# One more warm-up matmul ahead of the first transposes, and a full-width filler behind them

## The chip, the cores and the metric

The kernel runs on one core of one Trainium2 chip. The metric is device time in microseconds of a whole execution; it is some 1.9 us more than the span that a profile shows. All runs told of here come from several batches ("calls" in what follows), on different chips; the kernels compared with each other ran in the same rounds of one call. Two kernels count as the same within 2%.

## The reference, cut to what matters

One block of a network: a layer norm of x (2048 rows, 512 columns), then a local dilated attention (32 heads, window 8, dilation 2) and a gated MLP with a spatial 2048 x 2048 product, both added to x.

```python
xn = _layernorm(x, axis=-1)
return x + _A_ref(xn, A_wqkv, A_wo) + _B_ref(xn, B_w_in, B_w_sp, B_b_sp, B_w_out)

# in _B_ref:
z  = _gelu(jnp.einsum('bsd,df->bsf', x, w_in))
z2 = _layernorm(z[..., Fh:], axis=-1)
```

Only the very start bears on the change: the first four blocks of 128 rows of x are normalised, transposed, and multiplied with the second half of B_w_in, which comes in four pieces of 128 rows.

## The kernel before: the parts that matter

The kernel lists its work as tasks, and a scheduler in the program fixes each engine's order from estimated times (`est`) before anything is built. The filler multiplies ones by ones into PSUM bank 7; nobody reads the result. Cuts are marked with dots.

```python
def filler(n, name, est, prio=None, reads=(), w=512):
    def warm(t):
        last = None
        for i in range(n):
            last = t.matmul(ps[:, 3584: 3584 + w], nc.const_aps.tensor(1.0, [128, 128], BF),
                            nc.const_aps.tensor(1.0, [128, w], BF), start=True, stop=True)   # L637
        return last
    T("pe", warm, reads=reads, writes=[("ps", 7)], est=est, name=name, prio=prio)

filler(cfg["warm"], "warm", 400.0 * cfg["warm"])          # warm = 8
...
# first_wave(): block 0 in two halves, centred only; the scale is applied later
for h in range(2):
    ce(0, 256 * h, 256, ("xc0", h), "ab"[h])               # VectorE, L681
    xt(0, (k0, k1)[h], (2 * h, 2 * h + 1), ("xc0", h), "ab"[h])   # TensorE transposes, L694
    T("act", ...)                                          # ScalarE eviction, L710
filler(cfg["fill0"], "fill0", 216.0 * cfg["fill0"], reads=(("xc0", 1),), w=256)
...
z2_mm(*u[0], (0, 1))            # block 0, needs pieces 0 and 1 of B_w_in, L935
xt(1, kx, range(4), "xc1")
...
z2_mm(*u[1], (0, 1))
z2_mm(*u[0], (2, 3))            # "the eight" begin here: need pieces 2 and 3
z2_mm(*u[2], (0, 1))
z2_mm(*u[3], (0, 1))
z2_mm(*u[1], (2, 3))
...
xt(2, k2, range(4), ("xn", 2))  # VectorE's normalised blocks 2 and 3, L676
...
xt(3, k, range(4), ("xn", 3))   # "the last transposes" in what follows
```

Blocks are counted from zero in this code; the texts written before the runs say "third block of x" for number 2 and "ninth" for number 8.

Of the kernel before, what the change touches and what calls it, by code (L numbers as in the profile page):

```python
# [14 lines left out]
class Plan:  # L15
# [299 lines left out]
    tmap=1,  # L315
    xdma=4,
    fill=1,
    warm=8,
    fill0=1,
    acc=1,  # L320
    first_plain=0,
# [3 lines left out]
def build_kernel(nc, A_x, A_wqkv, A_wo, B_x, B_w_in, B_w_sp, B_b_sp, B_w_out, out, report=False, sched_kw=None,  # L325
                 cfg=None, emit=True):
    cfg = dict(DEFAULT_CFG, **(cfg or {}))
# [71 lines left out]
    with ExitStack() as es:  # L399
# [120 lines left out]
        def c_act(n, psum=True, accum=False):  # L520
            return 165.0 + n * (0.84 if psum else 0.84) + (110.0 if accum else 0.0)

        def c_dve(n, mode=1.0):
            return 155.0 + n / (0.96 * mode)
# [3 lines left out]
        def T(eng, fn, **kw):  # L528
            t = plan.add(eng, fn, **kw)
            if eng == "pe" and not t.name.startswith(("warm", "fill", "xTr", "red")):  # L530
                pe_seq.append(t)
            return t
# [100 lines left out]
# [8 lines that stand above are left out]
# [21 lines left out]
        def first_wave():  # L662
            dv = []

            def bn(b):
                dv.append(T("dve", lambda v: v.bn_stats(Fv("st6", 6, 9 * b), A("xin", 512, 512 * b)), reads=[("xin", b)],
                            writes=[("st6", b)], est=690, name="bnst%d" % b))
# [39 lines left out]
            for h in range(2):  # L707
# [4 lines left out]
                    ps[:, 512 * (k0, k1)[h] + 256 * h: 512 * (k0, k1)[h] + 256 * h + 256].rearrange("p (c n) -> p c n", c=2),  # L712
                    ACTF.Copy))(h),
                  reads=[("ps", (k0, k1)[h])], writes=["xcT0" + "ab"[h]], est=c_act(256), name="xTe0" + "ab"[h])
            filler(cfg["fill0"], "fill0", 216.0 * cfg["fill0"], reads=(("xc0", 1),), w=256)
            bn(1)
            ag(1)
            ce(1, 0, 512, "xc1")
# [8 lines left out]
            for b in range(2):  # L727
# [7 lines left out]
              reads=[("ps", kx)], writes=["xcT1"], est=c_act(512), name="xTe1")  # L735
# [10 lines left out]
            for b, hf, k in u[2:]:  # L746
# [6 lines left out]
                reads=[("ps", k)], writes=[("xnT", 3)], est=c_dve(512), name="xTe3"))  # L753
# [326 lines left out]
        def v_wave(j):  # L1080
            for b in range(4 * j, 4 * j + 4):
                v_block(b)

        first_wave()
        setup_masks()
        qk_wave(0)
# [8 lines left out]
          reads=["bia"], writes=["bdf"], est=170, name="bdf")  # L1095
# [330 lines left out]
```

## Time and profile before

| | kernel before |
|---|---|
| time, median of the 3 first runs | 233.64 us (233.41 to 233.75) |
| span of the profiled execution | 231.0 us |
| TensorE busy, by the page | 226.5 us, 98% |

The chain of waits and TensorE's timeline are quoted in the prediction. Three points in time are enough to read every run below: when TensorE's array becomes fast, when the eight of L935 start, and when the last transposes of the first wave start (9.59 us in this profile). What "fast" means can be read from the starts of matmuls of 512 columns: among the warm-ups, from 1.22 to 3.78 us, they come (3.78 - 1.22)/6 = 0.427 us apart, and the 32 of L809, from 12.85 to 19.75 us, 0.216 us apart. The trace's record of the granted clock puts the change at 4.04 us. In the recorded texts "cold" is the slow spacing and "warm" the fast one.

One more view of this profile is the part of the timeline that shows VectorE (start, length, engine, line, operation, and in brackets the idle time before it with the releaser):

```profile
7.35 0.69 DVE L666 BATCH_NORM_STATS2 fpool<-arena 128x6 f32<-128x512 bf16 x1
7.95 0.40 DVE L676 TENSOR_SCALAR arena<-arena,fpool 128x512 bf16<-128x512 bf16 x1
8.27 0.19 DVE L670 BATCH_NORM_AGGREGATE fpool<-fpool 128x2 f32<-128x9 f32 x1
9.12 0.41 DVE L676 TENSOR_SCALAR arena<-arena,fpool 128x512 bf16<-128x512 bf16 x1 [0.67 <-POOL fpool L672]
```

### The profile page before, as it was taken

The numbers are of one execution on the slowest core, as the hardware profiler recorded it, in microseconds if no ns is written. First come the engines' busy times: TensorE is split into PE (matmuls) and PEld (weight loads), VectorE is DVE, ScalarE is ACT, GpSimd is POOL, SyncE is SP. The second block draws the span as 40 slices with busy tenths as digits, with TensorE's granted clock in tenths as the row PEclk, the third lists the DMA queues.
The fourth block names the chain that finished last, engine by engine and source line by source line (L and its number), as shares of the span: only waits on it lengthen the run. The fifth ranks groups of instructions, "written<-read, shape, count | busy, mean of one in ns | idle before, by whom it ended". The sixth has DMA issues, their size and how long they took to land.

```text
span 231.0 us, 3311 instructions
## 1 busy us (share of the span) xinstructions
PE 226.5 (98%) x1236; PEld 111.3 (48%) x1236; DVE 205.7 (89%) x237; ACT 129.3 (56%) x235; POOL 43.3 (19%) x74
## 2 busy tenths in 40 slices
PE   7999999999999999999999999999999999999995
PEld 2444445444434565555545454454544544544442
DVE  4688879998998999999999999999999989999920
ACT  3698658978889996447662243324423433255311
POOL 4647959628026001000000000000000000000000
PEclk9999999999999999999999999999999999999999
DMA  6995989784109200459618999999999664946082
GB/s 224 261 289 114 163 206 327 222 225 141 45 23 198 74 3 0 76 109 223 210 37 175 214 218 249 272 226 296 220 244 232 146 206 92 284 111 137 11 168 65
DMA packets 77887, 38.90 MB, mean 168 GB/s; under 512 B 66220, under 2 KB 76332, under 8 KB 76848
## 3 DMA queue, kind: packets, MB, share of 16 engines
q1 hardware_dynamic: 71488, 31.89, 60.7%
q10 hardware_dynamic: 5568, 4.69, 7.0%
q0 software_dynamic: 816, 2.12, 3.1%
q8 instruction: 9, 0.15, 0.3%
q14 instruction: 6, 0.05, 0.1%
HBM read 18.49 MB, written 4.21 MB: 98 GB/s over the span
## 4 chain that ended last, share of the span: by engine, by line
PE 96%; DMA 2%; SPq 1%; issue 0%; ACT 0%
PE ps L1159 37%; PE ps L1278 16%; PE ps L809 12%; PE ps L966 11%; PE ps L935 10%; PE ps L789 6%; PE ps L848 3%; DMA arena<-in_B_w_in_dram 2%; SPq L602 0%; PE ps L694 0%; SPq L611 0%; ACT arena L1120 0%
## 5 line engine op out<-in xcount | busy, mean ns | idle before, releaser
L1159 PE MATMUL ps<-arena 128*128 128x448 bf16 x448 | 90.6, 352 | 0.0
L1159 PEld LDWEIGHTS ps<-arena 128*128 128x128 bf16 x448 | 43.8, 98 | 42.8 <-ACT arena L1120 0.3
L1278 PE MATMUL ps<-arena 128*128 128x512 bf16 (+2 forms) x187 | 43.9, 366 | 0.0
L1227 DVE TENSOR_TENSOR arena<-arena 128x4096 bf16<-128x4096 bf16 x16 | 36.6, 2286 | 0.3
L835 DVE TENSOR_TENSOR arena<-arena 128x4096 bf16<-128x4096 bf16 x16 | 36.2, 2279 | 0.0
L1236 DVE TENSOR_TENSOR arena<-arena 128x4096 bf16<-128x4096 bf16 (+2 forms) x24 | 33.6, 1402 | 1.1 <-DMA arena<-arena 0.2
L1120 ACT ACTIVATE arena<-ps 128x512 bf16<-128x512 f32 (+2 forms) x23 | 13.0, 564 | 36.2 <-PE ps L1159 25.4
L809 PE MATMUL ps<-arena 128*128 128x512 bf16 x128 | 28.6, 379 | 0.0
L1278 PEld LDWEIGHTS ps<-arena 128*128 128x128 bf16 x187 | 17.9, 98 | 18.5
L935 PE MATMUL ps<-arena 128*128 128x448 bf16 x128 | 25.7, 352 | 0.5 <-issue 0.3
L966 PE MATMUL ps<-arena 128*128 128x448 bf16 x128 | 24.8, 353 | 0.0
L1052 DVE TENSOR_TENSOR arena<-arena 128x1024 bf16<-128x1024 bf16 x32 | 21.0, 683 | 0.3
L809 PEld LDWEIGHTS ps<-arena 128*128 128x128 bf16 x128 | 12.4, 98 | 15.3 <-issue 0.4
L966 PEld LDWEIGHTS ps<-arena 128*128 128x128 bf16 x128 | 14.4, 114 | 10.2 <-issue 0.8
L972 ACT ACTIVATE arena<-ps 128x896 bf16<-128x896 f32 x16 | 14.4, 915 | 8.7 <-PE ps L966 8.7
L817 ACT ACTIVATE arena<-ps 128x1024 bf16<-128x1024 f32 x16 | 16.3, 1021 | 4.5 <-PE ps L809 4.0
L935 PEld LDWEIGHTS ps<-arena 128*128 128x128 bf16 x128 | 12.2, 98 | 12.3 <-issue 0.6
L943 ACT ACTIVATE arena<-ps 128x448 bf16<-128x448 f32 x28 | 15.1, 549 | 2.1 <-PE ps L935 0.3
L977 ACT ACTIVATE arena<-arena 128x896 bf16<-128x896 bf16 x16 | 15.1, 945 | 0.1
L789 PE MATMUL ps<-arena 128*128 128x512 bf16 x64 | 15.0, 379 | 0.0
L1168 ACT ACTIVATE ps<-ps,fpool 128x448 f32<-128x448 f32 x16 | 9.7, 604 | 8.5 <-PE ps L1159 8.5
L1120 ACT ACTIVATE ps<-arena 128x512 f32<-128x512 bf16 (+2 forms) x17 | 9.8, 576 | 5.5 <-ACT arena L1120 5.1
(74 smaller groups left out, 200.4 us busy)
## 6 DMA issues: line engine op xcount, KB each, us to landing
arena<-vscr SPq DMA_DIRECT2D x8, 1152.0 KB, 6.6
arena<-in_A_x_dram ACTq DMA_DIRECT2D x18, 128.0 KB, 3.6
vscr<-arena POOLq DMA_DIRECT2D x16, 128.0 KB, 3.7
arena<-in_A_x_dram SPq DMA_DIRECT2D x14, 128.0 KB, 3.1
out_dram<-arena ACTq DMA_DIRECT2D x14, 128.0 KB, 2.4
arena<-in_A_wqkv_dram SPq DMA_DIRECT2D x3, 512.0 KB, 4.9
arena<-in_B_w_in_dram SPq DMA_DIRECT2D x1, 896.0 KB, 4.9
arena<-in_B_w_out_dram SPq DMA_DIRECT2D x1, 896.0 KB, 6.7
```

Of the source, the lines that this page charges most:

```text
L789: last = t.matmul(bank(k), AC(off["xnT"] + dc * S + 128 * b, [[1, 128]]), AC(off["wv_raw"] + 512 * dc, [[1, 512]]), start=(dc == 0), stop= ...
L809: last = t.matmul(bank(k + which), AC(off["wqk"] + 1024 * dc + col0, [[1, 128]]), AC(off["xnT"] + dc * S + 512 * j, [[1, 512]]), start=(dc ...
L817: T("act", lambda a: a.activation(AC(qo, [[ko - qo, 2], [1, 512]]), ps[:, 512 * k: 512 * k + 1024].rearrange("p (t n) -> p t n", t=2), ACT ...
L835: T("dve", lambda v: v.tensor_tensor(pbv, qb, kb, ALU.mult), reads=rd, writes=[("pb", s_)], est=c_dve(4096, 2.0), name="prod%d_%d" % (j, c ...
L935: last = t.matmul(ps[:, 512 * k: 512 * k + HF], AC(xo, [[1, 128]]), AC(off["w_in2"] + FH * dc + HF * hf, [[1, HF]]), start=(dc == 0), stop ...
L966: last = t.matmul(ps[:, 512 * (k + hf): 512 * (k + hf) + HF], AC(off["xnT"] + dc * S + t0, [[ts, 128]]), AC(off["w_in1"] + FH * dc + HF * ...
L1052: T("dve", (lambda o_, x_, y_: lambda v: v.tensor_tensor(o_, x_, y_, ALU.subtract))(o_, x_, y_), reads=rd, writes=[wr], est=c_dve(NK * 128 ...
L1120: T("act", lambda a: a.activation(out_, in_, ACTF.Copy), reads=reads, writes=writes, est=c_act(n), name=name)
L1159: last = t.matmul(half(bk), lh(k), rh(k), start=(new and k == 0), stop=(k == NK - 1), skip_group_check=True)
L1227: T("dve", (lambda tv, iv, av: lambda v: v.tensor_tensor(tv, iv, av, ALU.mult))(tv, iv, av), reads=[("attn", j)] + ([("Ve", par)] if q < 2 ...
L1236: T("dve", (lambda o_, n: lambda v: v.tensor_tensor(o_, two(0, n), two(n, n), ALU.add))(o_, n), reads=[] if n > 512 else ["Vs", ("Ve", par ...
L1278: last = t.matmul(po, lh, rh, start=False, stop=(q == len(order) - 1), skip_group_check=True)
```

## The change

The intent is that TensorE should not stand idle around the first transposes (0.40 us before them and 0.29 us before the first L935 in this profile), so that the array becomes fast early. That idle time there delays this moment, the profile before doesn't show.

```diff
-    warm=8,
+    warm=9,
...
-            filler(cfg["fill0"], "fill0", 216.0 * cfg["fill0"], reads=(("xc0", 1),), w=256)
+            filler(cfg["fill0"], "fill0", 216.0 * cfg["fill0"], reads=(("xc0", 1),))
```

## The prediction

> **What bounds the kernel now.** I started with the page's chain of work that ended last, because it says which engine a saved nanosecond has to be saved on.
>
> ```profile
> PE 96%; DMA 2%; SPq 1%; issue 0%; ACT 0%
> ```
>
> TensorE carries 96% of the span of 231.0 us, so the kernel is TensorE-bound; the DMA's 2% must be somewhere at an end. The same chain in order of time shows where:
>
> ```profile
> 1.71 0.42 SPq L602
> 2.14 0.04 issue
> 2.18 4.69 DMA arena<-in_B_w_in_dram
> 6.87 0.14 issue
> 7.00 1.67 PE ps L935 x8
> 8.68 0.22 PE ps L694 x4
> 8.90 0.76 PE ps L935 x4
> 9.66 0.33 PE ps L694 x4
> ...
> 217.90 10.40 PE ps L1278 x59
> 228.32 0.28 ACT arena L1120
> ```
>
> The reader is to see two things. Up to 6.87 us the path is not TensorE at all: it is the issues on the sync engine's queue and one load of B_w_in, issued at 2.18 and landed 4.69 us later. From 7.00 to about 228.3 us it is TensorE without a break. Whatever TensorE does before 7.00 us matters only if it makes the eight matmuls at 7.00 start later, or if it changes the speed of what follows. The change touches two instructions, and both lie before 7.00 us. So the third view is the timeline of TensorE alone for the first microseconds (start, length, what, and in brackets the idle time before it and who ended it):
>
> ```profile
> 0.84 3.45 PE L637 MATMUL ps<-const-bfloat16-1.0 128*128 128x512 bf16 x8 [0.84 <-PEq L1411]
> 4.69 0.39 PE L694 MATMUL ps<-arena 128*128 128x128 bf16 x4 [0.40 <-DVE arena L681]
> 4.92 0.27 PE L637 MATMUL ps<-const-bfloat16-1.0 128*128 128x256 bf16 x1
> 5.49 0.54 PE L935 MATMUL ps<-arena 128*128 128x448 bf16 x2 [0.29 <-issue]
> 6.05 0.40 PE L694 MATMUL ps<-arena 128*128 128x128 bf16 x4
> 6.28 0.54 PE L935 MATMUL ps<-arena 128*128 128x448 bf16 x2
> 7.00 1.67 PE L935 MATMUL ps<-arena 128*128 128x448 bf16 x8 [0.18 <-DMA arena<-in_B_w_in_dram]
> ```
>
> Line 637 is the filler: eight 512-wide matmuls of ones ahead of the first transposes (L694), and one 256-wide one behind them. TensorE stands idle 0.40 us before the transposes, which wait for VectorE's centred input (L681); 0.29 us before the first real matmuls (L935); and 0.18 us before the eight at 7.00. The list of all waits of TensorE has only these and the 0.84 us at the very start. The 0.29 us is put down to issue there, but the weight load that goes ahead of those matmuls starts at 5.45 and was released by the B_w_in transfer after 0.49 us of idle time. So that wait too is the load's.
>
> [...] Seven of the eight warm-up matmuls are recorded with 634 ns and the eighth, which starts at 3.78 us, with 511. The mean start-to-start time is (3.78 - 0.84)/7 = 0.420 us[...]. The four transposes and what follows start 4.92 - 4.69 = 0.23 us apart, 57 ns each, which is warm. So in this execution the speed doubled during the eighth warm-up matmul, near 4.0 us. [...]
>
> **The change part by part.** Nothing is removed. The order of instructions on each engine was compared for both kernels: TensorE has the same rows, with the warm-up nine times instead of eight and the later filler 512 wide; the other four engines are identical. The semaphores and the PSUM bank of the filler are the same.
>
> 1. The ninth warm-up matmul. In the profiled execution the eighth is recorded to end at 3.78 + 0.51 = 4.29 us, and some 0.17 us of that is drain (379 ns for a warm 512-wide matmul in the L809 row less 216 of spacing), so the next could start near 4.12. Warm, it occupies 0.22 us, to 4.34. If it were cold it would start at 0.84 + 8 x 0.427 = 4.26 and occupy 0.43, to 4.69. The transposes start at 4.69 in any case, because VectorE decides it. On the path: 0 us, with 0.35 us to spare warm and none cold.
> 2. The wider filler. [...] Its recorded end moves from 4.92 + 0.27 = 5.19 to about 5.30. The next weight load, released by the transfer, is at 5.45 and its matmul at 5.49. On the path: 0 us, with some 0.2 us to spare.
> 3. A shift that got through either place would still have the 0.18 us of waiting at 7.00 to disappear in. There is another small reserve at 9.59: the last of the four sets of transposes needs VectorE's L676, which ends at 9.12 + 0.41 = 9.53, while the matmuls before it were through streaming at 8.74 + 4 x 0.189 = 9.50.
> 4. The clock. In this execution it was fast from about 4.0 us on, three microseconds before the path reaches TensorE. Nothing is left to gain here.
>
> The sum for an execution like the profiled one is 0.00 us. TensorE's busy time should rise by about 0.5 us, and its idle time fall by the same.
>
> **The rivals.**
> - *A late clock in the timed runs.* [...] For it: the profiled execution took 233.02 us and the three timed ones 233.41 to 233.75, some 0.4 to 0.7 more[...]. Against it: the three agree within 0.34 us[...], and profiled and timed runs may differ for other reasons. This would give 232.9 to 233.4 us.
> - *The added work gets in the way.* If the clock is still slow at 4.7 us, nine warm-ups end just where the transposes want to start, and the filler holds TensorE 0.43 instead of 0.21 us[...]. Going through it cold from 4.69: transposes 4 x 0.107 to 5.12, filler to 5.55 instead of 5.33, so the matmuls start up to 0.1 us after 5.45. Two of those take 0.75, transposes 0.43, two more 0.75: 7.48 against 7.38 before. So 0.1 us later: 233.7 us. For it: only that the margin in a cold run is nil. Against: the profiled clock was fast.
> - *A second wait takes over.* Even if TensorE were ready earlier at 5.49 or 7.00, the B_w_in pieces end both waits, and their issue and transfers hang on nothing that TensorE does. So filling idle time cannot pull the path forward. This is the main line, 233.6 us.
>
> **Range and chances.** The main line says 233.64 us unchanged, and I give it some 65%. The late clock, at 25%, would take off about 0.5; the harmful case, at 10%, adds about 0.1. The weighted mean is 233.64 - 0.125 + 0.01, so 233.5. The scatter of the runs before is 0.34 us, so a new median can move by 0.2 without any cause. From the rivals' ends and this scatter, the range is 232.9 to 234.0 us. 2% is 4.7 us[...], so both outer chances are 0.5%; same is 99%.
>
> **What would show it right or wrong.** In the changed kernel's timeline the eight matmuls of L935 should still start near 7.0 us with a wait for B_w_in before them, and be gap-free after it; the wait before the first transposes should shrink from 0.40 to about 0.2 us and the one before the first L935 from 0.29 to about 0.2; the span should stay within 0.3 us of 231.0. I am wrong if the eight start later although the load landed at the same time (the added work got in the way), or if the time falls by over 0.5 us while the trace of before shows nothing to gain (the late clock was real in the timed runs), or if warm-up matmuls of 634 ns are seen beyond the eighth followed by slow matmuls after 7.00[...].

The sum came to 0.00 us. One of its terms is the time of the 256 further columns in step 2; half of the 0.216 us spacing of L809 puts it at 0.11 us, and as it lay beside the path it counted 0 in the sum. The first rival came to cost about 1 us at most, with which the 4.7 us of 2% were compared: that was the estimate and was not shown.

The other figures of the steps can be followed from the trace. The 0.427 us of step 1 is the slow spacing named above, and the second rival scales it by width: 0.107 us for 128 columns, 0.75 for two of 448. Later runs show both, 107 ns in the profile after (from 4.63 us) and 3.73 us for ten of 448 in warm5 (from 6.86 us). The 0.17 us that step 1 calls drain is what the recorded length in L809 (379 ns) exceeds the spacing by (216 ns).

## The result, and the profile after

The changed kernel took 233.72 us (median of 6 runs, 233.01 to 233.97); the kernel before took 233.52 us in 6 runs (232.88 to 234.32). The ratio is 1.0, with a 95% interval of 0.9975 to 1.0025: the same. Ratios here are the mean time of one kernel's runs over that of the other's in the same rounds, so they are not quite the ratio of the medians.

The span of the profiled execution is 231.2 us. First the busy line of the page, before and then after:

```profile
PE 226.5 (98%) x1236; PEld 111.3 (48%) x1236; DVE 205.7 (89%) x237; ACT 129.3 (56%) x235; POOL 43.3 (19%) x74
```

```profile
PE 225.9 (98%) x1221; PEld 111.7 (48%) x1237; DVE 206.2 (89%) x237; ACT 129.3 (56%) x235; POOL 42.8 (19%) x74
```

The weight loads show the added matmul (1237 against 1236). TensorE's busy time seems to fall by 0.6 us, but only because 16 matmul records are missing from the second trace (1221 for 1237 weight loads). So the rise of 0.5 us that I had named as a check can't be read from this line.

TensorE's timeline after, answering to the one in the prediction:

```profile
0.84 4.00 PE L637 MATMUL ps<-const-bfloat16-1.0 128*128 128x512 bf16 x9 [0.84 <-PEq L1411]
4.63 0.62 PE L694 MATMUL ps<-arena 128*128 128x128 bf16 x4
5.06 0.41 PE L637 MATMUL ps<-const-bfloat16-1.0 128*128 128x512 bf16 x1
5.73 0.55 PE L935 MATMUL ps<-arena 128*128 128x448 bf16 x2 [0.26 <-DMA arena<-in_B_w_in_dram]
...
7.23 1.69 PE L935 MATMUL ps<-arena 128*128 128x448 bf16 x8 [0.35 <-DMA arena<-in_B_w_in_dram]
...
9.73 0.39 PE L694 MATMUL ps<-arena 128*128 128x128 bf16 x4
```

The idle time before the transposes is gone, and what lies before the first L935 is a wait for B_w_in (0.26 us). The eight start 0.23 us later than in the profile before, and they still waited 0.35 us for their load. In the chain of waits after, the same load took longer:

```profile
2.18 5.00 DMA arena<-in_B_w_in_dram
```

It was 4.69 us before, from the same issue at 2.18 us. The load accounts for the whole shift of the eight: 0.31 us later landing against a start 0.23 us later. Of the 0.23 us, 0.09 us went in the reserve at the last transposes (9.73 against 9.59), and the span grew by 0.17 us. So no part of the later end, between these two traces, is the work of the fillers.

A second thing differs: the transposes start 5.06 - 4.63 = 0.43 us apart from the filler behind them, 107 ns each, where before it was 57. The array was still slow, and it became fast at about 5.1 us instead of 4.04. So more warm-up went with a later clock in this pair, which the experiments take up.

### The profile page after: what moved, and what is told of

Read it like the earlier page. It is cut to its first block, busy times and chain, and to the rows that moved or that the text cites. A ratio compares the mean times of both kernels' runs of the same rounds, so it can differ in the third digit from the quotient of the medians.

```text
span 231.2 us, 3297 instructions
## 1 busy us (share of the span) xinstructions
PE 225.9 (98%) x1221; PEld 111.7 (48%) x1237; DVE 206.2 (89%) x237; ACT 129.3 (56%) x235; POOL 42.8 (19%) x74
## 3 DMA queue, kind: packets, MB, share of 16 engines
q10 hardware_dynamic: 5568, 4.69, 6.7%
## 4 chain that ended last, share of the span: by engine, by line
PE 95%; DMA 2%; issue 1%; SPq 1%; ACT 0%
PE ps L1159 37%; PE ps L1278 16%; PE ps L809 12%; PE ps L966 11%; PE ps L935 10%; PE ps L789 6%; PE ps L848 3%; DMA arena<-in_B_w_in_dram 2%; SPq L602 0%; PE ps L694 0%; SPq L611 0%; ACT arena L1120 0%
## 5 line engine op out<-in xcount | busy, mean ns | idle before, releaser
L1278 PE MATMUL ps<-arena 128*128 128x512 bf16 (+2 forms) x178 | 42.1, 366 | 0.5
L835 DVE TENSOR_TENSOR arena<-arena 128x4096 bf16<-128x4096 bf16 x16 | 36.2, 2280 | 0.0
L809 PE MATMUL ps<-arena 128*128 128x512 bf16 x124 | 27.9, 379 | 0.4 <-issue 0.2
L935 PE MATMUL ps<-arena 128*128 128x448 bf16 x128 | 25.7, 353 | 0.6 <-DMA arena<-in_B_w_in_dram 0.6
L809 PEld LDWEIGHTS ps<-arena 128*128 128x128 bf16 x128 | 12.3, 98 | 15.4 <-issue 0.7
L935 PEld LDWEIGHTS ps<-arena 128*128 128x128 bf16 x128 | 12.2, 98 | 12.6 <-DMA arena<-in_B_w_in_dram 1.4
L789 PE MATMUL ps<-arena 128*128 128x512 bf16 x61 | 14.7, 379 | 0.3 <-issue 0.2
```

Of the source, the lines that this page charges most:

```text
L789: last = t.matmul(bank(k), AC(off["xnT"] + dc * S + 128 * b, [[1, 128]]), AC(off["wv_raw"] + 512 * dc, [[1, 512]]), start=(dc == 0), stop= ...
L809: last = t.matmul(bank(k + which), AC(off["wqk"] + 1024 * dc + col0, [[1, 128]]), AC(off["xnT"] + dc * S + 512 * j, [[1, 512]]), start=(dc ...
L835: T("dve", lambda v: v.tensor_tensor(pbv, qb, kb, ALU.mult), reads=rd, writes=[("pb", s_)], est=c_dve(4096, 2.0), name="prod%d_%d" % (j, c ...
L935: last = t.matmul(ps[:, 512 * k: 512 * k + HF], AC(xo, [[1, 128]]), AC(off["w_in2"] + FH * dc + HF * hf, [[1, HF]]), start=(dc == 0), stop ...
L1278: last = t.matmul(po, lh, rh, start=False, stop=(q == len(order) - 1), skip_group_check=True)
```

## The experiments

In every variant the order of each engine's other instructions was kept as in the kernel before and compared. Where the number of fillers changed by much, the estimate given to the scheduler stayed at that of eight, since otherwise work far behind moves too. The kernel before ran in the same rounds.

Two theories stood at the start. Mine: both additions lie beside waits that end when a load or VectorE says so. Rival 1 (late clock): in some executions the array becomes fast late, which costs time, and the change cures it. Rival 2: the added work gets in the way.

### The two halves of the change, each alone

```diff
 # warm_only
-    warm=8,
+    warm=9,
 # fill_only
-            filler(cfg["fill0"], ..., reads=(("xc0", 1),), w=256)
+            filler(cfg["fill0"], ..., reads=(("xc0", 1),))
```

> Only the ninth warm-up matmul is added; the filler behind the transposes stays 256 wide. Main theory (both additions lie beside waits for VectorE and for the load of B_w_in): time within 0.3 us of before, the eight matmuls of L935 start where that load lets them, near 7.0 to 7.2 us. Rival 1 (the array often becomes fast late in timed runs, and the extra matmul cures it): 0.3 to 0.5 us faster. Rival 2 (the extra matmul delays the transposes and the delay reaches the end): about 0.1 to 0.2 us slower, with the eight of L935 starting later than their load.

> Only the filler behind the first transposes is made 512 wide. Main theory: time within 0.3 us of before; the filler is through streaming by about 5.15 us warm or 5.5 us cold, and the next matmuls wait for the load of B_w_in to 5.45 us or later. Rival 2 (in the way): about 0.1 us slower. Rival 1 (late clock): no more than 0.1 us faster, as only 0.1 us of idle time is filled. [...]

The ninth warm-up alone took 233.52 us against 233.43 (ratio 1.0005, 0.9972 to 1.0039), the wide filler alone 233.61 us (1.0009, 0.9979 to 1.0038). Both are the same as before, as the main theory has it. The profiles bear it out: the eight of L935 started at 8.00 and 7.43 us after waits of 1.04 and 0.49 us, both ended by B_w_in (first warm_only, then fill_only):

```profile
8.00 1.67 PE L935 MATMUL ps<-arena 128*128 128x448 bf16 x8 [1.04 <-DMA arena<-in_B_w_in_dram]
```

```profile
7.43 1.69 PE L935 MATMUL ps<-arena 128*128 128x448 bf16 x8 [0.49 <-DMA arena<-in_B_w_in_dram]
```

The load landed at 7.91 us in the first, a whole microsecond later than in the kernel before, though nothing of the change touches it. The array became fast at 3.9 us with nine warm-ups and at about 5.5 us with eight, so here the smaller number was the later one. Each kernel also had one run over 235 us (235.34 and 235.20), of which more below.

### Next to no fillers

```diff
-        filler(cfg["warm"], "warm", 400.0 * cfg["warm"])
+        filler(1, "warm", 3200.0, w=64)
 ...
-            filler(cfg["fill0"], ..., w=256)
+            filler(cfg["fill0"], ..., w=64)
```

> Both fillers are cut to one matmul of 64 columns each, everything else in the same order. If the fillers earn their keep by having the array fast when the path reaches TensorE: the matmuls before 7 us run cold, the eight of L935 start near 7.4 us instead of 7.0[...]; worked out, 0.41 us of late start and half of the cold time after 7.4 us, less 0.1 us of reserve before the last transposes: 0.5 to 2.2 us slower, middle 1.1. Rival (the ramp costs nothing here, because the start is bound by loads and VectorE anyway): within 0.3 us of before.

The sum came to 0.5 to 2.2 us. That slow time costs half of itself is the two spacings' doing (0.427 and 0.216 us).

234.35 us against 233.43, ratio 1.0031 (1.0006 to 1.0056): slower by about 0.7 us, in the expected range. TensorE's timeline:

```profile
4.66 0.61 PE L694 MATMUL ps<-arena 128*128 128x128 bf16 x4 [3.60 <-DVE arena L681]
...
5.61 0.90 PE L935 MATMUL ps<-arena 128*128 128x448 bf16 x2 [0.30 <-ACT arena L710]
6.31 0.63 PE L694 MATMUL ps<-arena 128*128 128x128 bf16 x4
6.74 3.25 PE L935 MATMUL ps<-arena 128*128 128x448 bf16 x10
...
10.80 0.39 PE L694 MATMUL ps<-arena 128*128 128x128 bf16 x4
```

The two matmuls at 5.61 take 0.70 us to the next start, where the same two take 6.12 - 5.73 = 0.39 in the profile after, and the transposes at 6.31 start 107 ns apart instead of 57. Most of the ten at 6.74 are slow too. Ten at 189 ns (the spacing of the 16 of L935 from 9.82 us on in the profile before) would be 1.9 us to the next start; here it is 9.82 - 6.74 = 3.08 us. The last transposes start 1.21 us later than in the profile before and the span is 1.2 us longer; that profile is an early one among those with eight (table below), so the 0.7 us of the timed runs is the better measure. So the fillers as a whole do earn their keep here; one more of them doesn't (1.0005 for warm_only).

### Fewer and more warm-up matmuls

```diff
-        filler(cfg["warm"], "warm", 400.0 * cfg["warm"])
+        filler(16, "warm", 3200.0)      # warm16;  warm12 and warm5 with 12 and 5
```

> Sixteen warm-up matmuls instead of eight, order of all else frozen. This measures where added work stops being free. Eight or nine run cold, the rest at 0.216 us each, so the transposes start at 5.8 to 6.35 us instead of 4.69, the first L935 0.75 us after that, the eight 0.98 us after those: 7.5 to 8.1 us instead of 7.0. Less 0.1 us of reserve: 0.4 to 0.9 us slower, middle 0.6, and the eight of L935 no longer wait for the load. Rival (slack ahead of the path is over 1 us, or something later takes the delay up): within 0.3 us of before.

> Twelve warm-up matmuls instead of eight. With the array fast at 3.5 to 5.6 us the last streams until 5.0 to 5.9 us, the first L935 starts 0.75 us after that and the eight 0.98 us later: 6.7 to 7.6 us, where the load of B_w_in landed at 6.9 to 7.9 us. So most of four extra matmuls should still be hidden: 0.0 to 0.3 us slower in the mean. Rival (the added work of the change is hidden only just, with no room): four extra matmuls cost close to half of what eight extra did, 0.3 us, in every run.

> Five warm-up matmuls instead of eight, order of all else frozen. They end at 0.84 + 5 x 0.427 = 2.97 us, so TensorE idles 1.7 us before the transposes. If [...] (3.5 to 5.6 us in the runs with eight and nine, 9.0 us with next to none), the array becomes fast later than with eight, most likely between 5 and 9 us, and the time is 0.0 to 1.1 us higher, middle 0.5. Rival (idle time before the transposes has no influence, five are as good as eight): fast at 3.5 to 5.6 us again, time within 0.2 us of before.

Sixteen took 234.04 us against 233.43 (1.0018, 0.9995 to 1.0041), which doesn't clear the scatter, but the trace shows the added work on the path:

```profile
0.84 5.05 PE L637 MATMUL ps<-const-bfloat16-1.0 128*128 128x512 bf16 x16 [0.84 <-PEq L1411]
5.73 0.38 PE L694 MATMUL ps<-arena 128*128 128x128 bf16 x4
...
6.48 0.55 PE L935 MATMUL ps<-arena 128*128 128x448 bf16 x2 [0.26 <-ACT arena L710]
...
7.09 2.16 PE L935 MATMUL ps<-arena 128*128 128x448 bf16 x10
...
10.07 0.39 PE L694 MATMUL ps<-arena 128*128 128x128 bf16 x4
```

The transposes now follow the warm-up without a gap. (They start at 5.73 us, a little before the 5.8 that I had given as the earliest.) The ten of L935 run through with no wait for the load between them, and the last transposes come 0.48 us later than in the profile before; the span is 0.6 us longer. Profiles with eight and nine warm-ups scatter as widely, so it isn't the 0.48 us that decides, but the chain of waits of this profile, which now begins with the fillers and not with the load:

```profile
0.84 5.05 PE ps L637 x16
```

In this execution rival 2 is right, at eight matmuls more. What it costs is not shown by the times.

Twelve took 233.41 us against 233.88 (ratio 0.9961, 0.9928 to 0.9993). I don't read that as a gain: in this call the kernel before had five of its eleven runs over 234.3 us, and 233.41 is no lower than the kernel before in other calls (233.29 to 233.6). It shows that four more matmuls cost nothing that the timing sees, against the rival of that run. The profile of this kernel tells more. Its array became fast only at 6.62 us, so all twelve ran slowly, and the chain of waits begins with them too:

```profile
0.84 5.28 PE ps L637 x12
```

The ten of L935 started at 7.45 us, so the eight among them at about 7.83 (two at 189 ns later), past the 6.7 to 7.6 us that I had expected. So no fixed number of fillers is free: how many fit ahead of the load depends on when the array becomes fast (at 3.74 us in warm16, 6.62 in warm12) and on when the load lands (at 6.87 us in the profile before, 7.91 in warm_only).

Five took 234.61 us against 233.88, with runs from 233.80 to 235.90 (ratio 1.0012, 0.9969 to 1.0056): undecided by time. In its profile the array became fast only at 11.02 us, later than the 5 to 9 us that I had expected, the last transposes started at 11.78 us, and the span was 233.1 us. That the rival's "five are as good as eight" fails is shown for this execution only.

### The two kernels once more

No edit: the kernel before and the changed one, as they are, for more profiles and times.

> The kernel before, unchanged, for a second profile and more times. Main theory: what differs from run to run is when the last piece of B_w_in and the later rows of x land (6.9 to 7.9 us for the former in the four profiles so far) and when the array becomes fast (3.5 to 5.4 us so far); the last four transposes of the first wave then start at 9.6 to 10.5 us, and the span is 221.4 us more than that, within 0.1 us unless another wait appears later. Rival (the scatter arises later in the kernel): spans that do not follow the start of the last transposes.

> The changed kernel, unchanged, for a second profile and more times. Main theory: same time as before within 0.3 us, the last transposes between 9.6 and 10.5 us and the span 221.4 us more. If the extra fillers fixed the moment at which the array becomes fast, it would be at 5.0 us again as in the first profile of this kernel[...].

In the same rounds before2 took 233.29 us and after2 233.26 (ratios to the kernel before of those rounds, 0.9991 and 0.9989). All profiles together, sorted by when the array became fast:

| run | warm-ups | array fast at | last transposes at | span | span less last transposes |
|---|---|---|---|---|---|
| early_load (below) | 8 | 3.46 | 10.95 | 232.3 | 221.4 |
| warm16 | 16 | 3.74 | 10.07 | 231.6 | 221.5 |
| warm_only | 9 | 3.90 | 10.49 | 231.9 | 221.4 |
| before | 8 | 4.04 | 9.59 | 231.0 | 221.4 |
| after3 (below) | 9 | 4.22 | 9.81 | 231.6 | 221.8 |
| decouple (below) | 8 | 4.76 | 9.80 | 232.3 | 222.5 |
| after2 | 9 | 4.87 | 9.44 | 231.6 | 222.2 |
| after | 9 | about 5.1 | 9.73 | 231.2 | 221.5 |
| fill_only | 8 | about 5.5 | 9.93 | 231.8 | 221.9 |
| before2 | 8 | 5.57 | 9.67 | 231.1 | 221.4 |
| warm12 | 12 | 6.62 | 10.43 | 231.9 | 221.5 |
| tiny_both | 1 small | 8.96 | 10.80 | 232.2 | 221.4 |
| x4_first (below) | 8 | 10.17 | 11.42 | 234.7 | 223.3 |
| warm5 | 5 | 11.02 | 11.78 | 233.1 | 221.3 |

The moments come from the trace's own record of the granted clock; for the two with "about", which lack it, from the spacing and length of the matmuls. (In the windows view that clock stands as 1.00 even for stretches where matmuls ran at the slow spacing, for instance from 3.34 to 6.76 us in x4_first, so it is the spacing that has to be read.) Two things follow. With eight warm-ups the moment lies at 3.5 to 5.6 us in five profiles and at 10.17 in a sixth (x4_first), with nine at 3.9 to 5.1 us in four: they overlap, so the number alone doesn't fix it. And nine of the fourteen spans are 221.3 to 221.5 us plus the start of the last transposes, whatever came before: from there on these nine run alike.

The other five lost 0.3 to 1.9 us more later on. My expectation for after2, a constant 221.4 us, failed by 0.8 us (its last transposes, at 9.44 us, also came before the 9.6 that I had given). The wait list of TensorE in that run shows one of the places, the reduction matmuls of L848 waiting for VectorE's products:

```profile
PE ps L848 <- DVE arena L835: 0.3, 1, 0.3
```

VectorE starts its second wave (L768) when later blocks of x land. In after2 it waited until 12.42 us for that, against 12.20 in before, and twice more for DMA transposes (0.51 and 0.68 us); its first L835 started at 24.52 instead of 23.34 us. So which chain ends last changes from run to run, in the same kernel.

### The last piece of B_w_in earlier

```diff
 # sync engine's queue
-   ldx0, ldw_in2_0, ldx2, ldw_in2_2
+   ldx0, ldw_in2_0, ldw_in2_2, ldx2
```

> The last piece of B_w_in is issued ahead of the third block of x on the sync engine's queue (they change places), nothing else. If TensorE's start hangs on that load alone, as the chain of waits has it: the eight of L935 start 0.2 to 0.5 us earlier than in the kernel before and the time falls by as much. My theory is that a second chain is as long: the rows of x, through VectorE's statistics and normalisation (L666 to L676), to the last transposes at 9.6 us and later. Then the third block of x lands later by about 0.4 us (224 KB at some 390 to 400 GB/s are 0.57 us, less what was in flight), its statistics start no earlier than 6.7 us, the last L676 ends no earlier than before, and the time is the same or up to 0.5 us slower, though the eight start earlier.

The 390 to 400 GB/s are from the windows view of the profile before: 399 from 3.6 to 4.0 us, 390 from 4.0 to 4.3, 396 from 5.0 to 5.5.

234.36 us against 233.60, ratio 1.0039 (1.0011 to 1.0067): slower by about 0.9 us, where I had allowed for 0.5 at most. TensorE's timeline and the load that VectorE waited for:

```profile
7.18 1.67 PE L935 MATMUL ps<-arena 128*128 128x448 bf16 x8 [0.50 <-DMA arena<-in_B_w_in_dram]
9.78 0.40 PE L694 MATMUL ps<-arena 128*128 128x128 bf16 x4 [0.92 <-DVE arena L676]
...
7.59 0.69 DVE L666 BATCH_NORM_STATS2 fpool<-arena 128x6 f32<-128x512 bf16 x1 [1.46 <-DMA arena<-in_A_x_dram]
```

The eight did not start earlier (7.18 us; both theories had expected that), so the load was not hastened in effect. But the third block of x landed at 7.57 us, its statistics began 1.35 us later than in before (6.24 us; I had expected some 0.4 us, and why it was so much more stays open), and TensorE then stood 0.92 us for L676. That is the second chain, shown as a bound by itself: with it late, an array that was fast from 3.46 us on is of no use.

### Both chains eased by order

```diff
 # TensorE: u[0] (2, 3) after u[2] (0, 1) and u[3] (0, 1)
-   z2_0_0_2, z2_1_0_0, z2_1_1_0, z2_0_1_2
+   z2_1_0_0, z2_1_1_0, z2_0_0_2, z2_0_1_2
 # VectorE
-   bnst3, norm2, bnag3, norm3
+   bnst3, bnag3, norm2, norm3
```

> Two changes of order alone, aimed at both chains: TensorE does the four matmuls of the second block that need only the first two pieces of B_w_in ahead of the two that need the last piece, and VectorE closes the fourth block's statistics (L670) before it normalises the third block, so that GpSimd's power runs beside the normalisation. If the two chains are the bound: the last L676 ends about 1.4 to 1.5 us after the fourth L666 began to be followed up, some 0.2 us earlier than in the kernel before, TensorE's wait for the load shrinks to 0.1 us or less, the last transposes start 0.05 to 0.2 us earlier, and the time is 0.0 to 0.3 us lower, which the timing can hardly show. If neither is the bound: no change of the last transposes' start.

233.33 us against 233.60, ratio 1.0001 (0.9974 to 1.0028): nothing gained. The wait before the eight was 0.31 us and was now ended by ScalarE's eviction (L733), not by the load, so the 0.1 us that I expected failed too. From the start of the fourth block's L666 to the end of the last L676 it took 9.60 - 7.54 = 2.06 us against 9.53 - 7.35 = 2.18 before; the saving was 0.12 us instead of 0.2. No version here beats the two kernels.

### A misjudged move, and a late clock

```diff
 # sync engine's queue
-   xTd0, ldx8, xTd1, ldx4, ldx5, ldx6, ldx7, ldwv, ...
+   xTd0, ldx4, xTd1, ldx5, ldx6, ldx7, ldwv, ldx8, ...
```

> On the sync engine's queue the fifth block of x is issued in the place where the ninth was, and the ninth after the V weights; nothing else. In the second profile of the changed kernel and in that of the reordered kernel, TensorE lost another 0.5 to 0.8 us after 12 us, with VectorE waiting for the fifth block to 12.4 and 13.1 us and L848 waiting for VectorE's L835. If that third chain (x block five, VectorE, first products) is a bound in some runs: the first L768 starts at 11.5 us or earlier instead of 12.2 to 13.1, TensorE has no wait for L835 at L848, the span is 221.4 us more than the start of the last transposes, and the mean time is 0.1 to 0.5 us lower. Rival (the losses after 12 us come from the DMA transposes and not from the load of x): waits for L835 or for DMA transposes remain and the time stays.

237.37 us against 233.88, ratio 1.0141 (1.0099 to 1.0184): 3.3 us slower, the reverse of what I expected. The fault was mine. VectorE's order, fixed by the scheduler, takes the ninth block before the fifth, so I had delayed the one that it waits for first.

```profile
15.99 1.29 DVE L768 BATCH_NORM_STATS2 fpool<-arena 128x6 f32<-128x512 bf16 x2 [3.46 <-DMA arena<-in_A_x_dram]
```

That was 12.20 us in before. So the third chain is real (the rows of x, delayed in this way, cost 3 us), but the run says nothing on the direction that I meant.

Its profile is worth more for another reason. Until 7.9 us this kernel is the kernel before, instruction by instruction, and its clock came late:

```profile
0.84 3.57 PE L637 MATMUL ps<-const-bfloat16-1.0 128*128 128x512 bf16 x8 [0.84 <-PEq L1416]
4.91 0.59 PE L694 MATMUL ps<-arena 128*128 128x128 bf16 x4 [0.50 <-DVE arena L681]
...
5.76 0.93 PE L935 MATMUL ps<-arena 128*128 128x448 bf16 x2
...
6.91 3.69 PE L935 MATMUL ps<-arena 128*128 128x448 bf16 x10
...
11.42 0.39 PE L694 MATMUL ps<-arena 128*128 128x128 bf16 x4
```

Eight warm-ups, then 0.50 us idle, and everything up to 10.17 us at the slow spacing: the transposes at 6.48 us start (6.91 - 6.48)/4 = 107 ns apart, where it is 57 in the profile before. The last transposes start 1.83 us later than in the profile before. By an estimate from the table, an execution of the kernel before with such an opening would take 221.4 + 11.42 + 1.9 = 234.7 us. That was not measured: the end of this run hung on the late rows of x.

### The changed kernel a third time

No edit.

> The changed kernel, unchanged, for more times beside the kernel before. In the profile of the kernel with the fifth block of x moved, whose first 7.9 us are those of the kernel before, the array became fast only at 10.17 us and the last transposes of the first wave started at 11.42 us, 1.6 us later than usual; a run of the kernel before with that would take about 235.2 us, and 3 of its 45 runs so far took 235.15 to 235.41 us. The changed kernel has none over 234.0 in 12 runs. If the extra fillers cure the late clock: again none of its six runs over 234.5 us, and the kernel before has one or so out of six over 234.5. If the change cures nothing: its runs over 235 are as frequent as those of the kernel before, so one in six is quite possible. The median is expected to be the same within 0.3 us either way; six runs can hardly settle it unless one over 235 appears.

233.63 us (233.18 to 233.94) against 233.47 (233.01 to 235.12), ratio 0.9995 (0.9968 to 1.0022). The kernel before again had one of eleven runs over 235 us, the changed one none.

The wait list of this profile puts the 0.62 us before the eight down to issue. It may have been the load's, as the 0.29 us was in the profile before; the views don't show it.

Over all, the kernel before has 56 runs, 13 over 234.0 us and 4 over 235; the changed kernel has 18, none over 234.0. The means are 233.69 and 233.46 us, the medians 233.55 and 233.44. With no difference between the kernels, none of 18 would fall among 13 such runs out of 74 with a chance of some 2%, but I chose the bound of 234.0 after seeing the times, and the runs are spread over different chips: three of the four over 235 us come from one call, in which the changed kernel was not run. In the three comparisons that time both kernels it is 5 of 34 against none of 18, a chance of some 11%. For the bound of 235 us, over all, the chance is 32%.

Nor is it shown that a late clock made the slow runs. Two of the four over 235 us are listed with a granted clock of 0.996 and 0.991, and that figure leaves a slow opening out (x4_first's profile, slow up to 10.17 us, has 1.0), so in these two the clock was low at some other time too; where, and whether it cost anything, is not on record. Beside the counts, what spoke for the change was an estimate of mine on how much work makes the array fast; no run shows that. No profile of the changed kernel shows a late clock like that of x4_first: its three became fast at 4.22, 4.87 and about 5.1 us. So it is open whether the change takes off the slow tail; if it does, that is worth about 0.1% in the mean and nothing in the median.

## Why the prediction was right, point by point

"Same" was the easy part: even next to no fillers moved the time by 0.3% only. What was tested is the mechanism.

- **The bound.** "From 7.00 to about 228.3 us it is TensorE without a break" held for the execution that I had, and the start hung on the load: the shift between the first two profiles follows the landing (0.31 us later) and not the fillers. What I underrated is that VectorE's chain is as long. I mentioned it as a "small reserve at 9.59". The move of one load (early_load) made this chain late, and that alone cost 0.9 us.
- **Step 1, the ninth warm-up.** Right in its sum, 0 us on the path. One clause was too strong: "The transposes start at 4.69 in any case". In the profile after, VectorE was ready earlier (their weight load was released at 4.41 us), and the ninth matmul, slow, held the first transpose to 4.63. That 0.2 us vanished in the waits for B_w_in at 5.73 and 7.23 us. A reading of the trace was wrong, without consequence: six of the eight warm-ups are recorded with 634 ns and the first with 586, not seven with 634.
- **Step 2, the wider filler.** Right: nothing on the path, alone (1.0009) and together.
- **Step 3, the reserves.** Right and measured: of the eight's 0.23 us later start, 0.09 us were absorbed at the last transposes. Twelve warm-ups, three more than the change has, still show no cost in the time. In the profiles of twelve and of sixteen the fillers are on the path.
- **Step 4, the clock.** "Nothing is left to gain here" holds for the profiled execution, not for all. The late clock of rival 1 exists: x4_first shows it with the opening of the kernel before. I had put its cost at about 1 us at most; in that profile it was 1.8 us at the last transposes, because the matmuls before 7 us run slow as well, which my sum left out: the slow matmuls ahead of the eight, 0.373 us each (the ten from 6.86 to 10.59 us in warm5), last until 6.91 + 2 x 0.373 = 7.66 us, and the weight loads that follow start at 7.71 us, where those of the eight start at 6.97 in the profile before. It was seen in one of six profiles with eight warm-ups. How often the timed runs have it isn't shown, and the median doesn't see it. Why I gave it 25% was also not right: the profiled execution's 233.02 us was an ordinary low run (the changed kernel has 233.01).
- **Rival 2** was seen on the path only with more work than was added, in the profiles with twelve and sixteen warm-ups, and in no time that is clear of the scatter.
- **Checks.** The eight near 7.0 us behind a wait for B_w_in (7.23) and the span within 0.3 us: as written. The wait before the first transposes should have shrunk to about 0.2 us and went to nothing, because the ninth matmul ran slow: this is the cold case of step 1, where I had counted on the warm one. The wait before the first L935 moved with the load. The rise of the busy time by 0.5 us can't be read, for the missing records, and was mis-added too: the two warm terms of steps 1 and 2 make 0.22 + 0.11 = 0.33 us. Of the signs of being wrong, only half of one came: the ninth warm-up was slow too, but no matmul after 7.00 us was.

## What to carry to other kernels

Added work that lay ahead of a wait which something else ended cost nothing here (ratios of 1.0005 and 1.0009), and for the same reason filling that idle time gained nothing: look at who ends the wait before counting the idle time as a gain. When the wait that matters ends with a transfer, look for a second chain of the same length before hastening it, and check in which order the consumer takes the pieces before moving a load. And where an effect comes in some executions only (here a late clock, in one of six profiles with eight warm-ups), the median can be blind to it; look at the slow tail, with a bound fixed beforehand and enough runs.

## What the traces show of the clock and of the loads

- Counted from the first matmul at 0.84 us, the array became fast after 2.9 us in warm16 and after 5.8 in warm12, both with no gap of 0.1 us or more between matmuls until then. With eight warm-up matmuls and the gaps behind them it came after 2.6 us (early_load) to 9.3 us (x4_first). What decides the moment is not shown; no run varied the busy time by itself.
- The largest delay of the last transposes against the profile before is 2.2 us, of a span of 231 (warm5, 11.78 us against 9.59).
- The landing of one and the same load varies between executions: the same issue at 2.18 us landed after 4.69 us (before), 4.94 (before2), 5.00 (after) and 5.73 (warm_only), all with that queue order, and the eight started at 7.00, 7.17, 7.23 and 8.00 us.
